# Convolution and mixture of experts on one core: the third round of fixed slots is merged into the per-expert tail

## The chip, the cores and the metric

The kernel runs on 1 core of one Trainium2 chip. The metric is device time in microseconds, the median of several runs. Besides, one execution is taken with the hardware profiler; its rows are what the prediction rests on. The span is the time from the first to the last instruction of that execution.

## The reference

What is computed is a causal depthwise convolution over the sequence (8 heads, 7 taps, taps made by a softmax) and then a mixture of 16 experts in 4 groups of 4, one expert per token:

```python
x = conv(x, softmax(weight))            # 8 x 2880 x 192 -> 23040 tokens of 192
g_idx = argmax(x @ w_group)             # group of each token, 4 groups
e_idx = argmax(xg @ w_expert[g])        # expert within the group, 4 experts
h  = maximum(xg[mask_e] @ w1[g, e], 0)  # 192 -> 1024
ye = h @ w2[g, e]                       # 1024 -> 192
out[tok_idx] = (g_w * e_w)[:, None] * ye
```

All is float32. The counts per expert are known only at run time; with the inputs here they lie between 1252 and 1628.

## The kernel before, in words

**Routing.** The 23040 tokens are routed in 25 units of 4 to 12 blocks of 120 tokens (`unit`). A unit convolves its tokens, writes rows of 196 values to `xcd` in HBM, computes logits and choices, and scatters the token numbers into per-expert lists in HBM (`idtab`, line 609). A unit is a Python generator; each `step` advances it by one small piece, so that routing work is put between the matmuls of the experts.

**Slots.** The expert work is a `plan` of slots. A slot takes up to 256 tokens of one expert: it gathers their rows by indirect DMA on POOL's queue (`gather`, line 674, one DMA per 128 rows, into one of four `xg` buffers), transposes them (`turn`, lines 689 and 690), multiplies with w1 (`hidden`, line 710) and w2 (`back`, lines 728 and 732), scales, and scatters into the output (`finish`, line 830, POOL's queue too). Each float32 operand is split in a rounded part and a remainder, so there are 5 matmuls per 128 hidden features and 2 per 128 rows and 128 features on the way back. ACT makes the rounded part, DVE the remainder.

**Portions and tail.** The plan before has three fixed portions, `portions = [(5, 1), (NU-6, 2), (NU, 1)]`: in the first, each expert has one slot of 256 rows (slots 0 to 15), which starts when 5 units are routed; in the second, two slots each (16 to 47); in the third, one slot each (48 to 63), which starts when all units are routed. What is left of each list goes to a tail of one entry per expert, the experts sorted by what they have left. An entry has a fixed shape (`PIECES`): pieces of 320, 384, 256 or 128 rows. The tail before holds 7040 rows in 25 pieces, from slot 64 to slot 88, in the order of `RANKS`. All in all 64 x 256 + 7040 = 23424 rows are computed.

**Pieces of the tail.** Pieces of 320 and 384 rows go through `hidden_wide` and `back_wide` (lines 787, 790, 793, 805, 811): the moving operand of w1's matmuls is 320 or 384 columns wide, each 128 features take a PSUM bank of their own, and the third row tile takes a bank of pool `pm`. Pieces of 128 rows go through `hidden_small`, `turn_small` and `back_small` (lines 746 to 772), which need extra transposes.

**Weights.** At each change of expert w1 and w2 are read again from HBM (`weights`, lines 623 to 626, SP's queue, 1.5 MB) and split (`split`, lines 638 to 651, on ACT and DVE).

**Opening.** `open_portion` reads the id lists of a portion (line 1070). For the last portion it also starts `open_tail`: the ends of the lists are padded (`close_table`, 16 writes at line 856, for which `seen` is made at line 849, an instruction kept in program order on DVE), the sorted table is computed on DVE, written and read back, and then the tail's ids are read (`tail_ids`, lines 1093 and 1095). `open_slot` advances this by one step per slot. `rate` sets how densely routing steps are put between matmuls: portion q's units are to be done `MARGIN` = 5 slots before that portion starts.

**Order.** Each engine and each DMA queue executes its instructions in the order in which the framework's scheduler put them. The scheduler works at build time from the program and its own estimate of when each instruction becomes ready, so that an instruction which waits for nothing by that estimate can stand far ahead of its place in the program. An instruction at the head of a queue whose input is not there holds everything behind it.

**In a slot** the order on TensorE is: first and second quarter of `hidden`, each followed by a part of the previous slot's `back`; the transposes for the next slot; then the third and fourth quarter of `hidden` in one run. The first matmul of that run is called the slot's mark below.

Of the kernel before, what the change touches and what calls it, by code (L numbers as in the profile page):

```python
# [35 lines left out]
def conv_moe_kernel(  # L36
# [20 lines left out]
    def pin(on, ins):  # L57
# [22 lines left out]
        [(320, 320)] * 2 + [(320, 256)] * 2 + [(256, 256)] + [(128, 320)] * 4 + [(384,)] * 3 + [(320,)] * 2 + [(256,)] * 2)  # L80
# [3 lines left out]
    RANKS = [5, 2, 6, 3, 7, 4, 8, 0, 9, 14, 1, 10, 12, 11, 13, 15]  # L84
    assert NTAIL == E and sorted(RANKS) == list(range(E)) and sorted(CAPS, reverse=True) == CAPS
# [18 lines left out]
    portions = [(NEED, 1), (NU - NEXT, 2), (NU, 1)]  # L104
# [12 lines left out]
    LAG_S = 2  # L117
# [162 lines left out]
    def clear_table():  # L280
        for h in range(2):
            pin(PINC1, nc.sync.dma_start(
                out=idtab[0:E * CAP, :].rearrange("(e r) c -> e (r c)", e=E)[:, h * LIM // 2:(h + 1) * LIM // 2],
                in_=fill[h * E:(h + 1) * E],
            ))
        pin(PINC2, nc.sync.dma_start(
            out=idtab[DUMMY:DUMMY + MOST, :].rearrange("(p r) c -> p (r c)", p=2), in_=fill[0:2, 0:MOST // 2],
        ))
# [325 lines left out]

    def weights(r1, r2, eng=None):
# [54 lines left out]
    def gather(ids, known, w=SLOT):  # L670
        xs = xg[nslot[0] % NXG]
        nslot[0] += 1
        for t, n in enumerate(split_rows(w)):
            nc.gpsimd.indirect_dma_start(  # L674
                out=xs[0:n, t, :], out_offset=None, in_=xcd[0:known, :],
                in_offset=bass.IndirectOffsetOnAxis(ap=ids[t].bitcast(U32), axis=0),
                bounds_check=known - 1, oob_is_err=False,
            )
# [58 lines left out]

    def hidden_small(W, X, h):
        xa, xb = X
        hp = ph.tile([P, 512], F32, name="ph")  # L740
        fs = slice(h * 512, (h + 1) * 512)
        xh, xl = xa[:, 0, 0:P], xa[:, 1, 0:P]
        ops = ((xh, W["ah"]), (xh, W["al"]), (xl, W["ah"]),
               (xb[:, 0, 0:P], W["bb"]), (xb[:, 1, 0:P], W["bb"]))
        for i, (xx, wgt) in enumerate(ops):
            nc.tensor.matmul(out=hp, lhsT=xx, rhs=wgt[:, fs], start=i == 0, stop=i == len(ops) - 1)
        hr = pa4.tile([P, UB, D2], F32, name="xcb").rearrange("p b d -> p (b d)")[:, 0:512]
        nc.scalar.activation(out=hr, in_=hp, func=AF.Relu)
        return hr

    def turn_small(hr):
        px = pm.tile([P, 512], F32, name="pm")
        for c in range(4):
            nc.tensor.transpose(px[:, c * P:(c + 1) * P], hr[:, c * P:(c + 1) * P], ident)
        hh = ff.tile([P, 2, SLOT], F32R, name="hh", bufs=HB).rearrange("p a b -> p (a b)")
        hl = ff.tile([P, 2, SLOT], F32R, name="hl", bufs=HB).rearrange("p a b -> p (a b)")
        nc.scalar.activation(out=hh, in_=px, func=AF.Copy)
        nc.vector.tensor_tensor(out=hl, in0=px, in1=hh.bitcast(F32), op=ALU.subtract)
        return hh, hl

    def back_small(W, oo, HH, h):
        hh, hl = HH
        cw = W["cw"]
        for c in range(4):
            f = 4 * h + c
            nc.tensor.matmul(
                out=oo[0][:, 0:2 * D], lhsT=hh[:, c * P:(c + 1) * P], rhs=cw[:, f].rearrange("p a d -> p (a d)"),
                start=f == 0, stop=False,
            )
        for c in range(4):  # L770
            f = 4 * h + c
            nc.tensor.matmul(
                out=oo[0][:, 0:D], lhsT=hl[:, c * P:(c + 1) * P], rhs=cw[:, f, 0, :], start=False, stop=f == NF - 1,
            )
# [263 lines left out]
    late = []  # L1038

    def open_tail():  # L1040
# [4 lines left out]
        for j in RANKS:  # L1045
            row = nc.values_load(
                tab[0][0:1, j, 2:3], engines=[ET.SP], min_val=0, max_val=DUMMY,
                skip_runtime_bounds_check_because=OOB_WHY,
            )
            tail_ids(row, idps["tail"][:, j], PIECES[j])  # L1050
            yield

    def open_portion(pi):
        need, spe = portions[pi]
        rows = spe * 2
        idp = const.tile([P, E, rows], I32, name=f"idp{pi}")
# [6 lines left out]
        else:  # L1063
# [42 lines left out]
    plan += [("tail", j, k) for j in RANKS for k in range(len(PIECES[j]))]  # L1106
# [4 lines left out]
    starts = {pi: i for i, (pi, e, s) in reversed(list(enumerate(plan))) if pi != "tail"}  # L1111

# [7 lines left out]
    assert not any(width(i) > SLOT and width(i + 1) < SLOT for i in range(len(plan) - 1))  # L1120

    def open_slot(i):
# [7 lines left out]
        while pi != "tail" and pi not in idps:  # L1130
# [6 lines left out]
        if late:  # L1137
            next(late[0], None)
# [107 lines left out]
    for i, (pi, e, s) in enumerate(plan):  # L1246
# [5 lines left out]
        n = min(w, SLOT) // P  # L1252
# [7 lines left out]
        oo = [po.tile([P, 512], F32, name="po") for _ in range(n)]  # L1260
        if w > SLOT:
            oo.append(None)
        steps = NF // 2 if n == 2 else 2
        for f2 in range(steps):
            last = f2 == steps - 1
            if w > SLOT:
                H2 = hidden_wide(W, turned[i], f2, w)

                def fold(W=W, oo=oo, H2=H2, f2=f2, w=w, xs=gathered[i], ids=ids, last=last):
                    if f2 == 0:  # L1270
                        oo[2] = pm.tile([P, 512], F32, name="pm")
                    back_wide(W, oo, H2, f2, w)
                    if last:
                        finish(oo, xs, ids, w)

                later(LAG - last, fold)
            elif n == 2:
                HH = hidden(W, turned[i], f2, lambda: advance(rate[0]))
                advance(rate[0])

                def fold(W=W, oo=oo, HH=HH, f2=f2, xs=gathered[i], ids=ids, last=last):
                    back(W, oo, HH, f2, lambda: advance(rate[0]))
                    if last:
                        finish(oo, xs, ids)

                later(LAG - last, fold)
            else:
                hr = hidden_small(W, turned[i], f2)

                def fold(W=W, oo=oo, hr=hr, f2=f2, xs=gathered[i], ids=ids, last=last):  # L1290
                    HH = turn_small(hr)

                    def fold2():
                        back_small(W, oo, HH, f2)
                        if last:
                            finish(oo, xs, ids, P)

                    later(LAG_S, fold2)

                later(0.5, fold)  # L1300
            if f2 == 0:
                open_slot(i + 2)
            for q in range(f2, NF // 2, steps):
                k = (q + 2) % 4
                if q < 2:
                    split_one(W, k)
                elif i + 1 < len(plan):
                    split_one(opened[i + 1][0], k)
            if i + 1 < len(plan):
                if f2 == n - 1:  # L1310
                    turned[i + 1] = turn(gathered[i + 1], width(i + 1))
# [30 lines left out]
```

## Time and profile before

| | |
|---|---|
| median of 3 runs | 1144.63 us (1143.6 to 1149.39) |
| profiled execution | 1137.87 us |
| its span | 1136.1 us |
| TensorE busy | 1087.7 us, 96% of the span |
| VectorE, ScalarE, GpSimd busy | 794.3, 719.6, 461.7 us |
| mean granted TensorE clock | 0.979 of full speed |
| DMA | 175.68 MB, mean 155 GB/s |

The profiled execution is 6.8 us shorter than the median of the runs, and its own time is 1.8 us more than its span. The rows below are all of this one execution. Times in them are microseconds from the span's start, "x" is a count, and a name such as L674 is a line of the program printed above.

### The profile page before, as it was taken

Reading aid. Unit: us, or ns where it says so; the run is one execution under the profiler, and the core shown is the slowest. Engines: PE = TensorE matmul, PEld = TensorE weight load, DVE = VectorE, ACT = ScalarE, POOL = GpSimd, SP = SyncE. Lnnn points to the kernel's source line nnn. Section 1 sums busy time; section 2 is a strip of 40 time slices with the busy share of each in tenths; the row PEclk is TensorE's granted clock in tenths of the full one; section 3 lists DMA queues with packets and bytes.
Section 4 is the critical chain, followed back from the end, with each engine's and each line's share of the span. In section 5 each row is a group of like instructions: output and inputs, shape, how many; then the busy total and the mean of one; then the engine's idle time right before and its main releaser. Section 6 shows DMA issues by size and latency. Waiting matters only on the chain. (4 is left out here: it accounts for less than half of the span.)

```text
span 1136.1 us, 23048 instructions
## 1 busy us (share of the span) xinstructions
PE 1087.7 (96%) x8170; PEld 1060.3 (93%) x8170; DVE 794.3 (70%) x1761; ACT 719.6 (63%) x1427; POOL 461.7 (41%) x420
## 2 busy tenths in 40 slices
PE   6799999999999999999999996999999999999995
PEld 5679899999999999999999996999999999999995
DVE  3747967887866666675678665888876766767772
ACT  4545576666775665656655664777776666666661
POOL 2003432234342534343435435555455454454531
PEclk9978999999999999999999998999999999999998
DMA  8879778879873564435354446777764444444420
GB/s 198 239 182 240 187 180 210 222 171 244 215 204 115 127 165 119 132 99 152 99 140 102 128 83 175 208 207 209 201 179 109 120 122 118 121 118 123 121 79 20
DMA packets 185203, 175.68 MB, mean 155 GB/s; under 512 B 47101, under 2 KB 166938, under 8 KB 185082
## 3 DMA queue, kind: packets, MB, share of 16 engines
q1 hardware_dynamic: 120108, 120.00, 39.2%
q0 software_dynamic: 18336, 36.08, 11.4%
q10 hardware_dynamic: 46638, 18.07, 7.4%
q8 instruction: 65, 1.06, 0.4%
q14 instruction: 56, 0.46, 0.1%
HBM read 138.23 MB, written 36.47 MB: 154 GB/s over the span
## 5 line engine op out<-in xcount | busy, mean ns | idle before, releaser
L728 PE MATMUL po<-cw,hh 128*128 128x384 f32 x1120 | 353.0, 372 | 0.4 <-ACT ys L822 0.4
L710 PE MATMUL ph<-xa,ah 128*128 128x256 f32 x1120 | 307.8, 296 | 4.4 <-DVEq L1190 2.4
L732 PE MATMUL po<-cw,hl 128*128 128x192 f32 x1120 | 281.2, 251 | 0.0
L715 ACT ACTIVATE hh<-ph 128x512 fp32r<-128x512 f32 x280 | 166.3, 595 | 162.7 <-PE ph L710 150.3
L674 POOL DMA_INDIRECT xg<-xcd,idp x128 | 143.1, 1118 | 306.6 <-ACT ys L822 275.6
L716 DVE SCALAR_TENSOR_TENSOR hl<-ph,hh 128x512 fp32r<-128x512 f32 x280 | 191.3, 686 | 92.9 <-ACT hh L715 89.7
L710 PE MATMUL ph<-xb,bb 128*128 128x256 f32 x1120 | 226.0, 283 | 0.0
L710 PEld LDWEIGHTS ph<-xa,ah 128*128 128x128 f32 x1120 | 212.3, 190 | 7.7 <-issue 2.7
L732 PEld LDWEIGHTS po<-cw,hl 128*128 128x128 f32 x1120 | 214.8, 192 | 1.9
L728 PEld LDWEIGHTS po<-cw,hh 128*128 128x128 f32 x1120 | 211.7, 189 | 2.9 <-ACT ys L822 0.6
L830 POOL DMA_INDIRECT out<-ys,idp x128 | 155.5, 1215 | 48.4 <-issue 30.1
L710 PEld LDWEIGHTS ph<-xb,bb 128*128 128x128 f32 x1120 | 173.2, 190 | 0.0
L710 PE MATMUL ph<-xa,al 128*128 128x256 f32 x560 | 158.3, 283 | 0.0
L822 ACT ACTIVATE ys<-po,xg 128x384 f32<-128x384 f32 x174 | 99.4, 581 | 77.2 <-PE po L732 41.5
L651 DVE TENSOR_TENSOR cw<-raw,cw 128x768 fp32r<-128x768 f32 x128 | 121.6, 952 | 19.3 <-ACT cw L650 17.4
L674 POOL DMA_INDIRECT xg<-xcd,idpt x61 | 69.2, 1135 | 136.7 <-ACT ys L822 95.2
L829 DVE TENSOR_TENSOR ys<-ys 128x192 f32<-128x192 f32 x177 | 62.6, 356 | 77.3 <-ACT ys L822 76.4
L650 ACT ACTIVATE cw<-raw 128x768 fp32r<-128x768 f32 x128 | 107.1, 842 | 4.2 <-DMA raw<-in_moe_w 4.1
L710 PEld LDWEIGHTS ph<-xa,al 128*128 128x128 f32 x560 | 107.5, 192 | 1.8
L639 DVE TENSOR_TENSOR al<-raw,ah 128x1024 fp32r<-128x1024 f32 x64 | 78.1, 1220 | 31.8 <-ACT ah L638 31.3
L830 POOL DMA_INDIRECT out<-ys,idpt x61 | 70.3, 1153 | 50.2 <-DVE ys L829 33.4
L638 ACT ACTIVATE ah<-raw 128x1024 fp32r<-128x1024 f32 x64 | 68.1, 1064 | 23.3 <-PE ph L710 10.1
(238 smaller groups left out, 1979.5 us busy)
## 6 DMA issues: line engine op xcount, KB each, us to landing
raw<-in_moe_w SPq DMA_DIRECT2D x128, 384.0 KB
raw<-in_moe_w SPq DMA_DIRECT2D x64, 512.0 KB
raw<-in_moe_w SPq DMA_DIRECT2D x64, 256.0 KB
xcd<-xc ACTq DMA_DIRECT2D x13, 742.5 KB
xin<-in_x SPq DMA_DIRECT2D x7, 1134.0 KB
xin<-in_x SPq DMA_DIRECT2D x6, 1039.5 KB
xcd<-xcb ACTq DMA_DIRECT2D x13, 360.0 KB
xg<-xcd,idp POOLq DMA_INDIRECT x128
```

Source lines behind the costliest of these rows:

```text
L638: pin(PINA, nc.scalar.activation(out=ah, in_=ra, func=AF.Copy))
L639: eng.get(k, nc.vector).tensor_tensor(out=al, in0=ra, in1=ah.bitcast(F32), op=ALU.subtract)
L650: pin(PINW, nc.scalar.activation(out=cw[:, fs, 0, :], in_=rc[k - 2], func=AF.Copy))
L651: eng.get(k, nc.vector).tensor_tensor(out=cw[:, fs, 1, :], in0=rc[k - 2], in1=cw[:, fs, 0, :].bitcast(F32), op=ALU.subtract,)
L674: nc.gpsimd.indirect_dma_start(out=xs[0:n, t, :], out_offset=None, in_=xcd[0:known, :], in_offset=bass.IndirectOffsetOnAxis(ap=ids[t].bitc ...
L710: nc.tensor.matmul(out=hp[:, j], lhsT=wgt[:, fs], rhs=xx, start=i == 0, stop=i == len(ops) - 1)
L715: nc.scalar.activation(out=hh, in_=hp, func=AF.Relu)
L716: nc.vector.scalar_tensor_tensor(out=hl, in0=hp, scalar=0.0, in1=hh.bitcast(F32), op0=ALU.max, op1=ALU.subtract,)
L728: nc.tensor.matmul(out=oo[t][:, 0:2 * D], lhsT=hh[:, j, ts], rhs=cw[:, f].rearrange("p a d -> p (a d)"), start=f == 0, stop=False,)
L732: nc.tensor.matmul(out=oo[t][:, 0:D], lhsT=hl[:, j, ts], rhs=cw[:, f, 0, :], start=False, stop=f == NF - 1,)
L822: nc.scalar.activation(out=y, in_=oo[t][0:n, 0:2 * D], func=AF.Copy, scale=g)
L830: nc.gpsimd.indirect_dma_start(out=outviews[nscat[0] % len(outviews)], out_offset=bass.IndirectOffsetOnAxis(ap=ids[t].bitcast(U32), axis=0 ...
```

## The change

The third fixed portion gets no slots of its own (`(NU, 0)`). Its 16 x 256 rows go into the tail, whose entries are now two or three pieces of 384, 320 and 256 rows, up to 896 rows per expert, 11136 rows in 36 pieces, from slot 48 to slot 83. Pieces of 128 rows and their functions are gone. The tail runs in order of size. The count of rows computed stays 48 x 256 + 11136 = 23424. The last portion now only closes the routing; its start is set to slot 48 - 8 = 40, so that routing is to end at slot 35, before 43. The tail's opening goes two steps per slot, and is forced on when a tail slot needs an id that is not read yet. The gather of a third row tile gets an order edge behind the gather of the second; the reads of the tail's ids get one behind the last w2 load issued so far.

```diff
     PIECES = (
-        [(320, 320)] * 2 + [(320, 256)] * 2 + [(256, 256)] + [(128, 320)] * 4 + [(384,)] * 3 + [(320,)] * 2 + [(256,)] * 2)
+        [(256, 384, 256)] * 2 + [(256, 320, 256)] * 2 + [(384, 384)] + [(384, 320)] * 4 + [(384, 256)] * 3
+        + [(320, 256)] * 2 + [(256, 256)] * 2)
...
-    RANKS = [5, 2, 6, 3, 7, 4, 8, 0, 9, 14, 1, 10, 12, 11, 13, 15]
...
-    portions = [(NEED, 1), (NU - NEXT, 2), (NU, 1)]
+    portions = [(NEED, 1), (NU - NEXT, 2), (NU, 0)]
+    LEAD = 8
...
-            hold(nc.sync.dma_start(
+            loads.append(nc.sync.dma_start(
                 out=rc[k], in_=w2f[bass.ds(r2 + k * HF * P, HF * P), :].rearrange("(f p) d -> p f d", p=P),
             ))
...
         for t, n in enumerate(split_rows(w)):
-            nc.gpsimd.indirect_dma_start(
...
+            with tc.issue_after(ins.ins) if t == 2 else nullcontext():
+                ins = nc.gpsimd.indirect_dma_start(
...
-        for j in RANKS:
-            row = nc.values_load(
...
-            tail_ids(row, idps["tail"][:, j], PIECES[j])
+        for j in range(NTAIL):
+            with tc.issue_after(loads[-1].ins):
+                row = nc.values_load(
...
+                tail_ids(row, idps["tail"][:, j], PIECES[j])
+            ready[0] = j + 1
             yield
...
-        else:
+        elif rows:
             ci = const.tile([1, E], I32, name=f"ci{pi}")
...
+    starts[len(portions) - 1] = len(starts) and plan.index(("tail", 0, 0)) - LEAD
...
-        if late:
-            next(late[0], None)
+        for _ in range(2):
+            if late:
+                next(late[0], None)
+        while pi == "tail" and ready[0] <= e:
+            next(late[0])
...
-        steps = NF // 2 if n == 2 else 2
-        for f2 in range(steps):
+        for f2 in range(NF // 2):
...
-                H2 = hidden_wide(W, turned[i], f2, w)
+                HH = hidden_wide(W, turned[i], f2, w, lambda: advance(rate[0]))
```

## Rows read from the trace of the kernel before

**Rows 1.** The page, part 1: busy us, share of the span, instructions, of each engine.

```profile
PE 1087.7 (96%) x8170; PEld 1060.3 (93%) x8170; DVE 794.3 (70%) x1761; ACT 719.6 (63%) x1427; POOL 461.7 (41%) x420
```

**Rows 2.** Windows by stage: stretch, length, busy us and records per engine, clock, DMA.

```profile
142.00:340.00 198.00, 197.57 (x1563) 191.65 (x1563) 152.49 (x315) 139.53 (x279) 74.30 (x65) 1.00 0.84 207
340.80:596.40 255.60, 255.60 (x2028) 252.36 (x2027) 169.88 (x351) 154.37 (x302) 101.86 (x93) 1.00 0.48 128
...
624.80:681.60 56.80, 56.80 (x445) 56.80 (x444) 38.06 (x62) 37.25 (x68) 22.06 (x20) 1.00 0.46 106
...
716.12:823.55 107.43, 107.43 (x838) 107.43 (x837) 90.44 (x132) 82.24 (x144) 55.76 (x43) 1.00 0.70 202
833.10:1023.17 190.07, 188.87 (x1313) 184.42 (x1311) 128.85 (x289) 126.42 (x252) 94.23 (x83) 1.00 0.44 124
```

**Rows 3.** Waits of PE over the span: what for, us in total, times, longest.

```profile
PE pm L689 <- DMA xg<-xcd,idp: 9.3, 2, 7.5
...
PE ph L710 <- DVEq L1190: 2.4, 1, 2.4
...
PE ph L787 <- DVE xc L793: 2.0, 7, 0.7
```

**Rows 4.** Timeline of POOL: start, us, instruction, idle before it and what ended it.

```profile
606.31 0.97 POOL L609 DMA_INDIRECT idtab<-lsi,rowi  x1 [2.29 <-DVE lsi L607]
...
686.14 0.99 POOL L674 DMA_INDIRECT xg<-xcd,idpt  x1 [14.83 <-DMA idpt<-idtab]
689.07 1.74 POOL L674 DMA_INDIRECT xg<-xcd,idpt  x1 [1.94 <-DMA idpt<-idtab]
691.11 1.02 POOL L674 DMA_INDIRECT xg<-xcd,idp  x1 [0.30 <-issue]
```

**Rows 5.** Timeline of SP's DMA queue, 590 to 712 us.

```profile
662.35 15.53 SPq L856 DMA_DIRECT2D idtab<-seen  x16
682.56 0.36 SPq L1093 DMA_DIRECT2D idpt<-idtab  x1
```

**Rows 6.** Waits of all engines, 660 to 715 us.

```profile
ACT cw L650 <- DMA raw<-in_moe_w: 4.1, 2, 2.1
```

**Rows 7.** Timeline of PE: the marks of slots 49, 50, 51 and 62, and two transposes.

```profile
685.28 0.30 PE L710 MATMUL ph<-xa,ah 128*128 128x256 f32 x1
...
694.30 0.33 PE L689 MATMUL pm<-ident,xg 128*128 128x128 f32 x1 [1.79 <-DMA xg<-xcd,idp]
...
702.21 0.47 PE L689 MATMUL pm<-ident,xg 128*128 128x128 f32 x1 [7.46 <-DMA xg<-xcd,idp]
...
706.33 0.30 PE L710 MATMUL ph<-xa,ah 128*128 128x256 f32 x1
...
716.12 0.30 PE L710 MATMUL ph<-xa,ah 128*128 128x256 f32 x1
...
823.55 0.30 PE L710 MATMUL ph<-xa,ah 128*128 128x256 f32 x1
```

**Rows 8.** Timeline of PE: marks in the tail (256 four times, 384 twice).

```profile
833.10 0.30 PE L710 MATMUL ph<-xa,ah 128*128 128x256 f32 x1
...
874.44 0.29 PE L710 MATMUL ph<-xa,ah 128*128 128x256 f32 x1
...
915.55 0.29 PE L710 MATMUL ph<-xa,ah 128*128 128x256 f32 x1
...
953.53 0.30 PE L710 MATMUL ph<-xa,ah 128*128 128x256 f32 x1
...
1061.00 0.35 PE L787 MATMUL ph<-xa,ah 128*128 128x384 f32 x1
...
1089.01 0.34 PE L787 MATMUL ph<-xa,ah 128*128 128x384 f32 x1
```

**Rows 9.** Groups by line, forms apart, DVE, 994 to 1108 us: busy us, mean ns.

```profile
L793 DVE SCALAR_TENSOR_TENSOR xc<-ph,xc 128x384 fp32r<-128x384 f32 x24 | 12.8, 552 | 4.5 <-ACT xc L790 4.1
...
L716 DVE SCALAR_TENSOR_TENSOR hl<-ph,hh 128x512 fp32r<-128x512 f32 x4 | 2.7, 686 | 1.6 <-ACT hh L715 1.6
```

More of the change, by code (lines that the diff above doesn't have):

```diff
@@ L1 @@
-from contextlib import ExitStack
+from contextlib import ExitStack, nullcontext
 import concourse.bass as bass
@@ L612, in unit @@
         finished(u)
+    loads = []
     def weights(r1, r2, eng=None):
@@ L735, in back @@
             hook()
[L738 to L774, printed above, removed]
     def hidden_wide(W, X, f2, w, hook=lambda: None):
@@ L1038, in conv_moe_kernel @@
     late = []
+    ready = [0]
     def open_tail():
@@ L1055, in open_portion @@
         rows = spe * 2
-        idp = const.tile([P, E, rows], I32, name=f"idp{pi}")
+        idp = rows and const.tile([P, E, rows], I32, name=f"idp{pi}")
         if pi == 0:
@@ L1105, in conv_moe_kernel @@
     plan = [(pi, e, s) for pi, (_, spe) in enumerate(portions) for e in range(E) for s in range(spe)]
-    plan += [("tail", j, k) for j in RANKS for k in range(len(PIECES[j]))]
+    plan += [("tail", j, k) for j in range(NTAIL) for k in range(len(PIECES[j]))]
     weights_at = {}
@@ L1129, in open_slot @@
                 open_portion(closing.pop())
-        while pi != "tail" and pi not in idps:
+        while (len(portions) - 1 if pi == "tail" else pi) not in idps:
             step()
@@ L1259, in conv_moe_kernel @@
             rare()
-        oo = [po.tile([P, 512], F32, name="po") for _ in range(n)]
-        if w > SLOT:
-            oo.append(None)
-        steps = NF // 2 if n == 2 else 2
-        for f2 in range(steps):
-            last = f2 == steps - 1
-            if w > SLOT:
-                H2 = hidden_wide(W, turned[i], f2, w)
-                def fold(W=W, oo=oo, H2=H2, f2=f2, w=w, xs=gathered[i], ids=ids, last=last):
+        oo = [po.tile([P, 512], F32, name="po") for _ in range(2)] + [None] * (w > SLOT)
@@ L1270, in fold @@
+        for f2 in range(NF // 2):
+            last = f2 == NF // 2 - 1
+            if w > SLOT:
+                HH = hidden_wide(W, turned[i], f2, w, lambda: advance(rate[0]))
+            else:
+                HH = hidden(W, turned[i], f2, lambda: advance(rate[0]))
+            advance(rate[0])
+            def fold(W=W, oo=oo, HH=HH, f2=f2, w=w, xs=gathered[i], ids=ids, last=last):
+                if w > SLOT:
                     if f2 == 0:
                         oo[2] = pm.tile([P, 512], F32, name="pm")
-                    back_wide(W, oo, H2, f2, w)
@@ L1273, in fold @@
[L1273 to L1281, printed above, removed]
-                    back(W, oo, HH, f2, lambda: advance(rate[0]))
[L1283 to L1300, printed above, removed]
+                    back_wide(W, oo, HH, f2, w, lambda: advance(rate[0]))
+                else:
+                    back(W, oo, HH, f2, lambda: advance(rate[0]))
@@ L1301, in conv_moe_kernel @@
+                if last:
+                    finish(oo, xs, ids, w)
+            later(LAG - last, fold)
             if f2 == 0:
                 open_slot(i + 2)
[L1303 to L1308, printed above, removed]
+            if f2 < 2:
+                split_one(W, f2 + 2)
+            elif i + 1 < len(plan):
+                split_one(opened[i + 1][0], f2 - 2)
```

23 lines of the change are left out of this document (10 added, 13 removed).

## The prediction

> **What bounds the kernel now.** I read the engines' shares first: TensorE (PE) is busy 96% of the span, the next engine 70% [rows 1]. PE sets the time, so a term of the sum must be either PE work that goes or PE idle time that goes. Then the table by stage. In the routing stages PE is busy 197.57 of 198.00 us and 255.60 of 255.60 us, in the slots 48 to 63 after a disturbance 107.43 of 107.43, in most of the tail 188.87 of 190.07 [rows 2]. So what isn't PE work sits in few places. The list of PE's waits names them: 9.3 us for two gathers, 2.4 us at the branch before the last slot, 2.0 us in seven short waits in the wide pieces (the longest 0.7) [rows 3]. The start of the kernel also has idle time, which the change doesn't reach.
>
> The 9.3 us are one event. The timeline of POOL shows at 686.14 a gather with tail ids (idpt) that had held the queue for 14.83 us until these ids landed, then another that held it for 1.94, and only then, at 691.11, the next gather with ordinary ids [rows 4]. Those ids are needed from slot 64 on, 14 slots later; the gathers stood early in the queue because nothing else held them back: a third row tile of an `xg` buffer has no earlier user. The ids were late because SP's queue was writing the 16 paddings from 662.35 for 15.53 us and read the first tail ids at 682.56 [rows 5]. Behind the two gathers stood those of slot 51, for which PE waits at the transposes 1.79 and 7.46 us [rows 7].
>
> **The change part by part.** The sum is made on the profiled execution, 1137.87 us, and its difference is carried to the median of 1144.63, which is 6.8 us higher.
>
> *Third tiles in order.* A slot undisturbed takes (823.55 - 716.12) / 11 = 9.77 us from mark to mark. From slot 49's mark to slot 50's it takes 706.33 - 685.28 = 21.05 [rows 7]. The event costs 21.05 - 9.77 = 11.28 us, of which 9.25 are the two waits; the other 2.0 go with the matmuls after them, which run at a lower granted clock (the transpose at 702.21 takes 0.47 us, that at 694.30 0.33). With the edge, a third tile's gather stands behind the second's, and that one waits for its buffer, so it can't run ahead. What is late next there is nothing in the rows: slots 51 to 62 run without a wait. **Term: -11.3 us.** Bounds: 0 (it stays) and -11.3.
>
> *Other pieces for the same rows.* 23424 rows in both. Before: 70 pieces of 256 (64 slots and 6), 12 of 320, 3 of 384, 4 of 128. After: 65, 8, 11 and none. So 5 x 256, 4 x 320 and 4 x 128 go, and 8 x 384 come (3072 rows each way). The prices come from marks in the tail [rows 8]. The order there is 128, 320, 320, 256 twice, then 128, 320, 256, 256. The first two groups take 41.34 and 41.11 us, the third 37.98. From the third, 128 + 320 cost 37.98 - 2 x 9.77 = 18.44. From the first two, 82.45 - 2 x 9.77 - 2 x 18.44 = 26.03, so 320 costs 13.0 (and 128 costs 5.4). Between two marks of 384 lie one 384 and one 320: 28.01 - 13.0 = 15.0 for 384. These prices have the waits of the tail in them. Removed: 5 x 9.77 + 4 x 18.44 = 122.6. Added: 8 x 15.0 = 120.0. **Term: -2.6 us.** A 384 is thus no cheaper by row than a 256 (1.5 x 9.77 = 14.65); what is gained is the dear 128s, with their extra transposes. Bounds: with 384 at 14.65, -5.4. On the other side, if each of the 19 wide pieces after met the longest wait seen, 0.7 us, instead of the mean of 2.0 / 15 = 0.13, 19 x 0.57 = 10.8 more, which gives +8.2. I take the marks, since they are the same pieces on the same engine.
>
> Against this stands a rule of the Trainium skill (VectorE: DVE Perf Modes, section "The TRN2 errata"): an operation has a fixed cost, so tiles should have 512 elements or more. What rows show first: DVE's remainder takes 686 ns for 512 columns and 552 for 384 [rows 9], so a 256 costs DVE 4 x 0.686 = 2.7 us of its 9.77, a 384 costs 8 x 0.552 = 4.4 of its 15.0, 28% and 29%. The rule shows in the price of one instruction, and by it alone the wide pieces would be the dearer ones, which is the third rival below; by the rows the load by time stays level.
>
> *Sixteen reloads of weights go* (25 MB, 16 times four loads on SP and eight splits on ACT and DVE). They lie beside PE: with a reload at each slot PE needs 107.43 / 838 = 128.2 ns for a matmul record, with one at each second slot 56.80 / 445 = 127.6 [rows 2]. The difference is 0.05 us a slot (76 records), 0.7 us for 16. **Term: -0.7.** Bounds 0 and -0.7.
>
> *Routing ends at slot 35 instead of 43.* The same PE work, denser: the last units are spread over 24 slots instead of 32. In the stage from 142 to 340 us routing is denser than it will be anywhere later (DVE is busy 77% there, 66% in the next), and PE is kept busy all the same [rows 2]. **Term 0**; the cover is that PE has work in any case. If that cover is gone, I have only the idle share of the denser stage, 0.43 of 198 us, as a price: under 0.6 us.
>
> *The tail's opening moves with it*, 16 paddings (15.53 us of SP's queue [rows 5]), the table on DVE, 32 id reads. Behind them on SP stand the weight loads. In the profile that block makes ACT wait 4.1 us for w2 [rows 6], and no PE wait for a weight follows [rows 3]; that was with a reload at each slot, while the block now falls on slots with one at each second, so the cover is wider. The 16 id reads of the third portion go from the same queue. The order edge behind w2 holds an id read until that load is issued; who waits for an id read is the gathers on POOL, and behind these all gathers and scatters. What it takes to be in time is the last rival. **Term 0**, bounds 0 and that rival's price.
>
> *Two gathers and two scatters fewer on POOL, 80 matmuls fewer on the w1 side:* within the prices above. *The end* (branch, last slot of 256, last scatter) stays, with its 2.4 us.
>
> Sum: -11.3 - 2.6 - 0.7 = -14.6 us, the profiled execution 1123.3, the median **1130**.
>
> **The rivals.**
>
> *The wait stays or comes back with the new first tail pieces.* The rows name the buffer, not the row tile, so that the two early gathers were third tiles is my reading of the program. If they weren't, or if other gathers take their place, only -2.6 - 0.7 is left: 1141.3. For it: the queue still mixes gathers whose ids come by two ways. Against it: a first or second tile has to wait for its buffer's earlier user. Chance 0.11.
>
> *The wide pieces are dear.* The upper bound above, 10.8 us: 1141. For it: 10 of the new wide pieces come one after the other (384, 384 and four times 384, 320), with splits of weights on DVE in the middle, and it is DVE that PE waits for [rows 3]. Against it: the same mix at 1061 to 1089 us is already in the price of 15.0. Chance 0.12.
>
> *Slower: the tail's ids come too late for slot 48.* Before, the third portion stood between the end of routing and the tail. From the last list scatter at 606.31 to the first gather with tail ids at 686.14 [rows 4] it takes 79.8 us. Slot 51's gather came to the head of POOL's queue at 686.14 - 14.83 = 671.3, 33 us ahead of that slot's undisturbed mark (685.28 + 2 x 9.77 = 704.8). So slot 48 needs the lists done 79.8 + 33 = 113 us, 11.6 slots, ahead: by slot 36.4. The plan is slot 35, and two steps per slot instead of one shorten the chain, whose longest part is the padding that waits for its place in the program. If routing ended where it does now, 69 us ahead of slot 48's mark (685.28 - 9.77 = 675.5), POOL would be held 44 us. PE had about 10 us of cover (19.8 us late on POOL, 9.3 idle on PE), so it would lose 34: 1164. It gets slower than before by over 0.5% when PE loses 14.6 + 5.7 = 20.3 us, which is a list done after slot 39.6. Chance 0.06.
>
> **How the numbers follow.** 0.5%, 5.7 us, is about what a measurement of this kernel can tell from no change. Forecast 0.71 (1123 to 1138), the wait stays 0.11, wide pieces dear 0.12, ids late 0.06. Low end: all bounds at their best, 11.3 + 5.4 + 0.7 = 17.4, and the fastest run shown being 1.0 below the median, give 1126; 1.2 us of PE idle in the tail [rows 2] and the scheduler's new order elsewhere can add a little, so 1123. High end: the two rivals at 1141. That leaves out the late ids and the tails of the rest, under 0.2. Faster by over 0.5% means under 1138.9: the forecast and half of the dear wide pieces, 0.77. Within it: the rest of these and the wait that stays, 0.17. Slower: 0.06.
>
> **What would show it.** Right: no gather with tail ids holds POOL for more than a few us, and PE's wait for gathers in the middle is gone; the stage after slot 48 needs about 15.0 us for a 384 and 9.77 for a 256; the paddings on SP stand some 60 to 110 us ahead of the first tail slot; PE's wait L787 for DVE is 2 to 4 us in all. Wrong: a hole in PE's 40 slices at the first tail pieces or at the end of routing; a wait of PE for weights after SP's block; a price of 384 over 15.5.

## The result, and the profile after

The changed kernel takes 1135.73 us (median, 1132.99 to 1136.54) beside 1147.01 for the kernel before. The ratio on record for this pair is 0.9874, interval [0.9825, 0.9922]; the quotient of the two medians, 0.9902, lies within it. Against the 1144.63 of the prediction, 1130 was forecast, a ratio of 0.9872. The experiments e1 to e4, e5 to e8 and e9 to e12 ran on a chip each; on the first and the last of these the ratio came out as 0.9841 [0.9808, 0.9873] and 0.9824 [0.9792, 0.9857]. So the kernel is faster, by 1.3 to 1.8% as these ratios have it. These ratios leave out one slow execution of e2, which took 4218.45 us. The size is near the forecast, though the last interval lies wholly on the faster side of it; most of the steps to it are not, as the experiments show.

The table of PE's waits of the changed kernel (what for, us in total, times, longest) has no row for gathers of 9.3 us any more [rows 3]:

```profile
PE ph L752 <- DVE xc L758: 6.4, 13, 1.1
...
PE ph L713 <- DVE hl L719: 3.3, 3, 2.1
...
PE ph L713 <- DVEq L1161: 1.0, 1, 1.0
```

L752, L713 and L1161 answer to L787, L710 and L1190 of before. POOL's timeline has the last list scatter and the first gather with tail ids [rows 4]:

```profile
538.29 0.96 POOL L609 DMA_INDIRECT idtab<-lsi,rowi  x1 [1.77 <-DVE lsi L607]
...
660.44 1.05 POOL L677 DMA_INDIRECT xg<-xcd,idpt  x1 [4.05 <-ACT ys L787]
```

No gather waits for tail ids now: the first that uses them waited for ACT's scaling of an earlier slot (`ys`, L787), which still read its buffer, and not for a DMA. The paddings stand at 578.45 on SP's queue and the first id read at 597.23, 98 and 80 us ahead of the first tail slot's transposes at 676.77 [rows 5]:

```profile
578.45 10.66 SPq L821 DMA_DIRECT2D idtab<-seen  x16
597.23 0.36 SPq L1061 DMA_DIRECT2D idpt<-idtab  x1
```

And yet this profiled execution spans 1134.3 us, only 1.8 less than the 1136.1 of before, with PE as busy as it was [rows 1]:

```profile
PE 1087.8 (96%) x8054; PEld 1060.3 (93%) x8054; DVE 728.8 (64%) x1652; ACT 666.5 (59%) x1338; POOL 453.0 (40%) x416
```

The reading needs stages. I cut each span at the first transpose for slot 5 and at that for slot 48 (the first slot of the third portion before, the first tail slot after; the rows left to compute are the same), in microseconds:

| kernel | up to slot 5 | slot 5 to 48 | slot 48 to end | span |
|---|---|---|---|---|
| before | 161.5 | 501.6 | 473.0 | 1136.1 |
| changed | 172.8 | 504.0 | 457.5 | 1134.3 |
| before again (e1) | 163.4 | 501.7 | 469.1 | 1134.2 |
| changed again (e2) | 163.4 | 502.6 | 451.1 | 1117.0 |
| before with the edge (e3) | 165.8 | 501.0 | 470.4 | 1137.2 |
| changed without the edge (e4) | 167.2 | 502.6 | 451.1 | 1120.9 |
| changed, routing late (e5) | 163.0 | 514.8 | 451.6 | 1129.3 |
| before, routing early (e6) | 162.3 | 514.8 | 459.7 | 1136.8 |
| before, early and edge (e7) | 164.8 | 506.1 | 461.4 | 1132.3 |
| changed, wide piece last (e8) | 162.2 | 502.8 | 448.6 | 1113.5 |
| changed, one weight load (e9) | 166.9 | 503.1 | 446.6 | 1116.6 |
| changed, table on GpSimd (e10) | 167.9 | 504.3 | 451.5 | 1123.7 |
| both (e11) | 170.0 | 503.5 | 452.9 | 1126.4 |
| changed again (e12) | 169.3 | 503.0 | 453.6 | 1125.9 |

The first profile of the changed kernel lost 11.3 us up to slot 5, where the order of PE's instructions is that of before. In e2, the same program, this part takes 163.4. It is a matter of the execution (more on it in the last section); the medians are over several executions. From slot 48 on the change saves 15.5 us in the first pair and 18.0 in the second; slots 5 to 48 cost 2.4 and 0.9 more.

### The profile page after: what moved, and what is told of

Same layout as the page of the kernel before. It is cut to its first block, busy times and chain, and to the rows that moved or that the text cites. A ratio compares the mean times of both kernels' runs of the same rounds, so it can differ in the third digit from the quotient of the medians.

```text
span 1134.3 us, 22263 instructions
## 1 busy us (share of the span) xinstructions
PE 1087.8 (96%) x8054; PEld 1060.3 (93%) x8054; DVE 728.8 (64%) x1652; ACT 666.5 (59%) x1338; POOL 453.0 (40%) x416
## 4 chain that ended last, share of the span: by engine, by line
PE 78%; DVE 6%; DMA 6%; issue 4%; ACT 3%; POOL 1%; another core or an unknown queue 1%; SPq 0%; POOLq 0%; ACTq 0%
PE ph L713 24%; PE po L731 15%; PE ph L752 8%; PE po L735 7%; PE po L770 4%; PE pm L437 4%; PE pm L485 2%; PE pm L770 2%; PE po L776 2%; DMA out<-ys,idpt 2%; PE pm L692 2%; DMA raw<-in_moe_w 2%; PE pm L693 2%; PE pm L455 1%; PE pm L480 1%
## 5 line engine op out<-in xcount | busy, mean ns | idle before, releaser
L731 PE MATMUL po<-cw,hh 128*128 128x384 f32 x1040 | 328.0, 372 | 1.1 <-ACT ys L787 1.1
L713 PE MATMUL ph<-xa,ah 128*128 128x256 f32 x1040 | 289.0, 298 | 6.2 <-DVE hl L719 3.3
L719 DVE SCALAR_TENSOR_TENSOR hl<-ph,hh 128x512 fp32r<-128x512 f32 x260 | 178.0, 688 | 138.2 <-ACT hh L718 121.5
L735 PE MATMUL po<-cw,hl 128*128 128x192 f32 x1040 | 261.0, 251 | 0.0
L677 POOL DMA_INDIRECT xg<-xcd,idp x96 | 110.3, 1149 | 260.0 <-ACT ys L787 228.7
L713 PE MATMUL ph<-xb,bb 128*128 128x256 f32 x1040 | 209.9, 284 | 0.0
L713 PEld LDWEIGHTS ph<-xa,ah 128*128 128x128 f32 x1040 | 198.8, 191 | 9.6 <-DVE hl L719 3.9
L677 POOL DMA_INDIRECT xg<-xcd,idpt x91 | 97.2, 1069 | 204.3 <-ACT ys L787 180.9
L713 PEld LDWEIGHTS ph<-xb,bb 128*128 128x128 f32 x1040 | 162.5, 192 | 0.0
L713 PE MATMUL ph<-xa,al 128*128 128x256 f32 x520 | 148.8, 286 | 0.0
L787 ACT ACTIVATE ys<-po,xg 128x384 f32<-128x384 f32 x168 | 96.3, 582 | 70.1 <-PE po L735 38.9
L795 POOL DMA_INDIRECT out<-ys,idp x96 | 116.0, 1208 | 39.6 <-issue 22.4
L795 POOL DMA_INDIRECT out<-ys,idpt x91 | 105.9, 1164 | 52.1 <-issue 28.3
L755 ACT ACTIVATE xc<-ph 128x384 fp32r<-128x384 f32 (+1 forms) x152 | 69.0, 468 | 84.5 <-PE ph L752 60.0
L758 DVE SCALAR_TENSOR_TENSOR xc<-ph,xc 128x256 fp32r<-128x256 f32 (+1 forms) x216 | 81.8, 415 | 54.9 <-ACT xc L755 49.4
L752 PE MATMUL ph<-xa,ah 128*128 128x384 f32 (+1 forms) x304 | 100.6, 334 | 6.4 <-DVE xc L758 6.4
L713 PEld LDWEIGHTS ph<-xa,al 128*128 128x128 f32 x520 | 99.9, 192 | 2.0
L653 DVE TENSOR_TENSOR cw<-raw,cw 128x768 fp32r<-128x768 f32 x96 | 91.5, 954 | 13.9 <-ACT cw L652 8.0
```

Of the source, the lines that this page charges most:

```text
L653: eng.get(k, nc.vector).tensor_tensor(out=cw[:, fs, 1, :], in0=rc[k - 2], in1=cw[:, fs, 0, :].bitcast(F32), op=ALU.subtract,)
L677: ins = nc.gpsimd.indirect_dma_start(out=xs[0:n, t, :], out_offset=None, in_=xcd[0:known, :], in_offset=bass.IndirectOffsetOnAxis(ap=ids[t ...
L713: nc.tensor.matmul(out=hp[:, j], lhsT=wgt[:, fs], rhs=xx, start=i == 0, stop=i == len(ops) - 1)
L719: nc.vector.scalar_tensor_tensor(out=hl, in0=hp, scalar=0.0, in1=hh.bitcast(F32), op0=ALU.max, op1=ALU.subtract,)
L731: nc.tensor.matmul(out=oo[t][:, 0:2 * D], lhsT=hh[:, j, ts], rhs=cw[:, f].rearrange("p a d -> p (a d)"), start=f == 0, stop=False,)
L735: nc.tensor.matmul(out=oo[t][:, 0:D], lhsT=hl[:, j, ts], rhs=cw[:, f, 0, :], start=False, stop=f == NF - 1,)
```

## The experiments

**Both kernels again.** No edit. 

> The kernel before, unchanged. Theory A (the 11.3 us by which the profile of after is behind at slot 5 is a matter of the execution, not of the change): the time by which the first transposes of slot 5 come is not 161.5 us again but up to 173, the rest of the span is as in the first profile (slot 48's transposes 501.6 us after slot 5's, the hole of some 21 us between the marks of slots 49 and 50 again), and the median of the runs stays 1143 to 1150. Rival B (the start is slower because of the change): slot 5's transposes stay at 160 to 163 us in this profile and the span at 1135 to 1138.

> The changed kernel, unchanged, for a narrower interval and a second profile. Theory A: ratio 0.986 to 0.990; in the profile slot 5's transposes come at any time from 161 to 173 us, and from slot 48's transposes to the end it takes 457 to 458 us. Rival B: slot 5's transposes at 172 to 174 us again.

Measured: 0.9987 [0.9964, 1.001] for the kernel before against itself, and 0.9841 for the change. The hole, as the stretch near slots 50 and 51 is called here in which PE stands and waits, is there in e1, on POOL (first fence) and on PE (second):

```profile
686.41 0.98 POOL L674 DMA_INDIRECT xg<-xcd,idpt  x1 [13.07 <-DMA idpt<-idtab]
```

```profile
700.73 0.48 PE L689 MATMUL pm<-ident,xg 128*128 128x128 f32 x1 [5.67 <-DMA xg<-xcd,idp]
```

From the transposes for slot 50 to those for slot 52 it takes 10.04 + 18.53 = 28.57 us in place of 2 x 9.76: the hole is worth 9.1 us here. So e1 to e2 is the cleanest pair: start 0.0, middle +0.9, from slot 48 on -18.0. The start does vary by itself (theory A). The 451.1 us of e2 from slot 48 on are fewer than the 457 to 458 expected: the first profile of the change has waits of ACT there (last section) that e2 doesn't have.

**The edge alone, and the change without it.**

```diff
+            with tc.issue_after(ins.ins) if t == 2 else nullcontext():
```

> The kernel before with the order edge for third row tiles alone; portions, pieces and routing as before. Theory (the edge takes the hole away, the prediction's term of 11.3 us): no gather with tail ids stands among those of slots 48 to 63, mark 49 to mark 50 takes 9.8 us, time 11.3 us under before, ratio 0.990. Rival (the hole is the padding's block of SP's queue, not the two gathers): PE still loses 5 to 11 us near slot 50 to weights that come late, ratio 0.995 to 1.000.

> The changed kernel without the order edge for third row tiles. Theory: third tiles of the first composites run ahead in POOL's queue, the first some 30 places before the first other tail gather, about 8 slots; it waits for ids that land at about 599 us, so POOL stands 10 to 20 us near 580 us and PE loses 5 to 12 us there; ratio 0.993 to 0.999. Rival (with the routing's end moved forward the ids are early enough, so the edge is worth nothing in this kernel): PE waits under 1 us for gathers, ratio 0.986 to 0.990.

Measured: e3 0.9995 [0.9975, 1.0014], e4 0.984 [0.9811, 0.9869], as much as the whole change. The edge does what it says and gains nothing. In e3 no gather with tail ids stands early in the queue, and the hole is still 5.2 us. SP's queue, ACT and PE in e3:

```profile
666.04 12.01 SPq L857 DMA_DIRECT2D idtab<-seen  x16
...
692.48 1.01 SPq L1094 DMA_DIRECT2D idpt<-idtab  x1
693.59 0.38 SPq L623 DMA_DIRECT2D raw<-in_moe_w  x1
```

```profile
697.46 1.06 ACT L638 ACTIVATE ah<-raw 128x1024 fp32r<-128x1024 f32 x1 [5.01 <-DMA raw<-in_moe_w]
```

```profile
703.45 0.39 PE L711 MATMUL ph<-xa,ah 128*128 128x256 f32 x1 [3.28 <-DVE hl L717]
...
847.29 0.33 PE L690 MATMUL pm<-ident,xg 128*128 128x128 f32 x1 [2.29 <-DMA xg<-xcd,idpt]
```

The paddings and the id reads behind them hold SP until 693; a w1 load comes out only then; ACT, at the head of whose queue the split of that weight stands, waits 5.01 us; behind it on ACT is the rounded part that DVE and then PE wait for. And the gathers that no longer run ahead are late at the tail's start: from one slot's transposes to the next it takes 16.80 us where e1 takes 12.76 (4.0 more). Hole and tail start together give back what the edge takes away. Of the two expectations the rival's came true.

In e4 the third-tile gathers do run ahead in the changed kernel, and one holds POOL:

```profile
591.53 1.04 POOL L677 DMA_INDIRECT xg<-xcd,idpt  x1 [11.15 <-DMA idpt<-idtab]
```

PE has no wait there, as the rival said. In the changed kernel the opening falls on slots of the second portion, which load weights at every second slot only, and the gathers are far enough ahead to bear 11 us.

**The routing's end.** e5 takes the lead away from the changed kernel, e6 gives it to the kernel before, e7 gives it lead and edge:

```diff
-    LEAD = 8
+    LEAD = 0
```

```diff
+    starts[len(portions) - 1] -= 8
```

> The changed kernel with LEAD = 0: routing is to end at slot 43 as before, all else as changed. Theory (the prediction's last rival: the tail's ids come too late for slot 48): the last list scatter comes some 70 us ahead of slot 48's mark instead of 137; from it to the first id read it took 59 us in the changed kernel, and the gather needs the ids 33 us ahead, so POOL is held 20 to 35 us and PE loses 10 to 25 us near slot 48; ratio to the kernel before 0.993 to 1.006. Rival (the end of routing has slack at 43 as well): no wait of PE for tail gathers, ratio 0.983 to 0.987.

> The kernel before with one line more: the third portion's start counts as slot 40, so that routing ends at slot 35; portions, pieces and gathers as before. Theory (the hole at slot 50 has two causes, one behind the other: gathers that wait for tail ids, and weights that are late behind the 16 paddings on SP; both come from the padding standing in the stage with a reload of weights at each slot): with the paddings 8 slots earlier the hole of 9 to 11 us is gone, ratio 0.990 to 0.993. Rival (the two gathers run ahead whatever the routing does): a hole of over 5 us moves to slots 40 to 45, ratio 0.996 to 1.000.

> The kernel before with the early end of routing and the order edge for third tiles. Theory: hole gone as in the run without the edge; what the edge alone gave back at the first tail pieces (the third tile's gather in line, 4 to 5 us near slot 64) is seen here again unless its ids are early; ratio 0.990 to 0.995, not better than without the edge. Rival (the edge is needed): clearly lower than without it.

Measured: e5 0.9955 [0.9939, 0.997], e6 0.9997 [0.9978, 1.0017], e7 0.9962 [0.9941, 0.9983]. In e5 a gather with tail ids stands at the head of POOL's queue (POOL's timeline):

```profile
608.07 0.97 POOL L609 DMA_INDIRECT idtab<-lsi,rowi  x1 [2.28 <-DVE lsi L607]
...
663.28 1.05 POOL L677 DMA_INDIRECT xg<-xcd,idpt  x1 [11.88 <-DMA idpt<-idtab]
```

But PE's one large wait, before the first tail slot's transposes at 677.74, is for an accumulator of `back` that ACT has to empty, and it isn't POOL that holds ACT (SP, then ACT, then PE):

```profile
644.66 10.76 SPq L821 DMA_DIRECT2D idtab<-seen  x16
660.73 0.36 SPq L1061 DMA_DIRECT2D idpt<-idtab  x1
661.62 0.36 SPq L625 DMA_DIRECT2D raw<-in_moe_w  x1
```

```profile
665.93 1.06 ACT L640 ACTIVATE ah<-raw 128x1024 fp32r<-128x1024 f32 x1 [12.33 <-DMA raw<-in_moe_w]
...
669.68 1.05 ACT L787 ACTIVATE ys<-po,xg 128x384 f32<-128x384 f32 x2
```

```profile
670.32 0.69 PE L731 MATMUL po<-cw,hh 128*128 128x384 f32 x1 [9.92 <-ACT ys L787]
```

The w1 load of the first tail entry stands on SP behind the paddings and the first id read, ACT waits 12.33 us for it, and what empties the accumulator (L787) comes after it on ACT. It is the chain of e3, longer. Slots 5 to 48 take 12.0 us more than in e8 on the same chip; PE has no wait for a gather with tail ids in this stretch. It might have had one: the first tail slot's gathers went out at 663.28 and 664.64, and its transposes were due at about 664.9 (from slot 47's transposes to these it takes 22.6 us in place of 9.76). That wait, if it is one, lies in the shadow of the weights'. In the changed kernel itself the w1 loads go out at 574.62, ahead of the paddings, and ACT has no wait for a weight there.

In e6 the hole moves with the opening, to slots 43 and 44, and stays (POOL, then PE):

```profile
610.89 0.99 POOL L674 DMA_INDIRECT xg<-xcd,idpt  x1 [12.25 <-issue]
```

```profile
621.88 0.33 PE L689 MATMUL pm<-ident,xg 128*128 128x128 f32 x1 [1.80 <-DMA xg<-xcd,idp]
...
635.50 0.48 PE L689 MATMUL pm<-ident,xg 128*128 128x128 f32 x1 [3.66 <-DMA xg<-xcd,idp]
```

These two slots take 8.5 us more than 2 x 9.76. POOL stood 12.25 us before a gather with tail ids; the trace names no releaser for it. So the theory of e6 failed and its rival held.

In e7 there is neither wait. So in the kernel before the hole goes only if the third tiles are held and the opening is moved. Why the move helps is read from how far ahead of the first transposes of its slot SP issues a w1 load: 14.3 us in slots 54 to 59 of the kernel before, which load at every slot, and 43.6 in slots 40 and 42 of the changed one, where every second slot loads. The first w1 load behind the block of paddings and id reads is still 2.45 us ahead in e3 (for slot 51), 40.1 in the changed kernel (for slot 44) and 24.5 in e7 (for slot 46; SP, then PE):

```profile
626.97 0.38 SPq L623 DMA_DIRECT2D raw<-in_moe_w  x1
```

```profile
651.45 0.27 PE L690 MATMUL pm<-ident,xg 128*128 128x128 f32 x1
```

In e5 the block stands in the same portion, but just ahead of the tail, and the load behind it was 3.3 us ahead of its slot. So few loads are not enough; what counts is that none is due soon behind the block. The order edge of the id reads behind a w2 load and the two steps per slot were not tried alone; e7 has neither and no hole.

That pair is worth 4.3 us (0.9962). In e7's profile 4.8 us of slots 5 to 48 are lost at slot 8, long before the opening (20.8 us, 15.9 in all other runs), so its stages show less than the 9.1 of the hole. The rest of the change's gain, 0.9962 to 0.984, is some 14 us by the ratios, which come from two chips. By the stages of e7 and e2 10.3 us of it fall to the merged tail, from slot 48 on; the other 3.5 lie before slot 48, where e7 lost its 4.8.

**The wide piece last in an entry.**

```diff
-        [(256, 384, 256)] * 2 + [(256, 320, 256)] * 2 + [(384, 384)] + [(384, 320)] * 4 + [(384, 256)] * 3
+        [(256, 256, 384)] * 2 + [(256, 256, 320)] * 2 + [(384, 384)] + [(384, 320)] * 4 + [(256, 384)] * 3
```

> The changed kernel with the wide piece as the last of an entry instead of the middle or first one (256, 256, 384; 256, 256, 320; 256, 384; 256, 320), same rows. Theory (the wide pieces came out cheaper than priced, 14.5 and 12.5 us instead of 15.0 and 13.0, because the splits of the next weights on DVE fall into 256 pieces): with the splits ah and bb in the wide pieces the nine entries cost 0.3 to 0.6 us more each, 3 to 5 us in all, ratio 0.987 to 0.989, and PE's wait L752 for DVE rises from 1.7 to over 4 us. Rival (the price depends on the width alone): ratio 0.983 to 0.985.

Measured: 0.983 [0.9804, 0.9856], not to be told from the change (0.984). The theory failed: PE's wait L752 falls to 0.9 us. By the stages the tail takes 448.6 us from slot 48 on, 2.5 less than in e2. Entries of three pieces take what they took. Those of two with one 256 got cheaper: (256, 384) 24.26 us where (384, 256) takes 24.46 in e2, and (256, 320) 22.29 where (320, 256) takes 23.13. The loads are the same. What moved is the place of their splits on DVE: of the four for each load, three (one of `bb` and the two of `cw`) have a remainder of the 256 next behind them (L719) in e8, and one of the wide piece (L758) in e2 (a split and what follows it, in e8 and then in e2):

```profile
1046.13 0.96 DVE L653 TENSOR_TENSOR cw<-raw,cw 128x768 fp32r<-128x768 f32 x1
1047.01 0.68 DVE L719 SCALAR_TENSOR_TENSOR hl<-ph,hh 128x512 fp32r<-128x512 f32 x1
```

```profile
1026.16 0.96 DVE L653 TENSOR_TENSOR cw<-raw,cw 128x768 fp32r<-128x768 f32 x1 [0.38 <-ACT cw L652]
1027.04 1.47 DVE L758 SCALAR_TENSOR_TENSOR xc<-ph,xc 128x256 fp32r<-128x256 f32 x6
```

**One weight load for the last eleven entries.** Their rows are computed with the weights of the fifth entry.

```diff
-            W = weights(...) if s == 0 else opened[i - 1][0]
+            W = weights(...) if s == 0 and e < 5 else opened[i - 1][0]
```

> The changed kernel without the weight loads and splits of the last 11 tail entries, which use the fifth entry's weights instead (so their rows get the wrong expert). In the changed kernel a 384 between two slots of 256 takes 14.5 us and a 320 there 12.5, 27.0 together, but the pair (384, 320), which has a load of weights within it, takes 27.53, and in the kernel before 384 and 320 with a load each take 28.0. Theory A: a load that falls on wide pieces costs PE about 0.5 us, since DVE's splits of weights stand in front of its remainders: the pairs go to 27.0, the entries (384, 256) from 24.46 to 24.27, in all -2.5 to -4 us against the changed kernel, ratio near 0.981. Theory B: it is two wide pieces in a row that cost the half microsecond: the pairs stay at 27.5, ratio that of the changed kernel, 0.984. Theory C (the prediction's): loads cost 0.04 us each wherever they fall, -0.5 us, pairs at 27.5.

Measured: the time, 0.9823 [0.9793, 0.9852], can't be told from that of e12 beside it, whose executions spread over 10 us. The stage can: from slot 48 on 446.6 us, against 451.1 (e2), 451.5 (e10) and 453.6 (e12). PE's transposes for four slots of 384, each a pair (384, 320) from the last, in e2 (first fence) and in e9 (second):

```profile
864.90 0.27 PE L692 MATMUL pm<-ident,xg 128*128 128x128 f32 x1
...
892.47 0.27 PE L692 MATMUL pm<-ident,xg 128*128 128x128 f32 x1
...
920.01 0.27 PE L692 MATMUL pm<-ident,xg 128*128 128x128 f32 x1
...
947.58 0.27 PE L692 MATMUL pm<-ident,xg 128*128 128x128 f32 x1
```

```profile
868.56 0.27 PE L692 MATMUL pm<-ident,xg 128*128 128x128 f32 x1
...
895.61 0.27 PE L692 MATMUL pm<-ident,xg 128*128 128x128 f32 x1
...
922.68 0.27 PE L692 MATMUL pm<-ident,xg 128*128 128x128 f32 x1
...
949.75 0.27 PE L692 MATMUL pm<-ident,xg 128*128 128x128 f32 x1
```

A pair takes 27.56 us with a load and 27.06 without. With two loads it took 28.01 in the kernel before [rows 8]. Each load that falls on wide pieces costs PE about half a microsecond in these pairs, theory A. Over the eleven loads taken away it is 4.5 us (e2 to e9), 0.4 each. Where it goes is seen in e2, on DVE and on PE:

```profile
898.11 0.96 DVE L653 TENSOR_TENSOR cw<-raw,cw 128x768 fp32r<-128x768 f32 x1
898.98 1.69 DVE L758 SCALAR_TENSOR_TENSOR xc<-ph,xc 128x384 fp32r<-128x384 f32 x3
```

```profile
898.99 0.36 PE L770 MATMUL po<-cw,xc 128*128 128x384 f32 x1
899.59 0.45 PE L752 MATMUL ph<-xa,ah 128*128 128x384 f32 x1 [0.24 <-DVE xc L758]
```

DVE splits a piece of w2 for 0.96 us, three remainders of the wide slot stand behind it, and PE's next matmul, due 0.2 us after the last start, comes after 0.6. In e9 PE's waits have no L752 row at all; in e2 they have eight, 1.7 us in all. This run takes away the transfers and ACT's splits too. That it is the order on DVE is shown by e8, which has every load: its (256, 384) and (256, 320) take 24.26 and 22.29 us, and in e9 (384, 256) and (320, 256) without a load take 24.27 and 22.29.

**The table's steps on GpSimd**, alone and with the wide piece last:

```diff
-                    ts(t["q"], t["rank"], k + 0.5, ALU.is_lt, float(XT), ALU.mult)
-                    tt(t["cap"], t["cap"], t["q"], ALU.add)
+                    nc.gpsimd.tensor_scalar(out=t["q"], in0=t["rank"], scalar1=k + 0.5, ...)
+                    nc.gpsimd.tensor_tensor(out=t["cap"], in0=t["cap"], in1=t["q"], op=ALU.add)
```

> The changed kernel with the 14 steps on capacities in the tail's table (two lines of the table, 16 values each) on GpSimd instead of DVE. Theory A: PE's 2.0 us wait for DVE's remainder at the end of routing, and the lower clock behind it, come from these DVE instructions standing in a block in front of the remainder: the wait goes to under 1 us, -2 to -3 us against the changed kernel, ratio near 0.9815. Rival: the other instructions of the table are enough to make the same wait, or the table is later and moves the paddings: 0 to -0.5 us, ratio 0.984.

> The changed kernel with the wide piece last in an entry and with the table's steps on GpSimd. If the two gains are independent (the first was 3 us, the second up to 3): 0.980 to 0.981; if the second is nothing: 0.983.

> The changed kernel once more, beside the other three on this chip, as the base for them: 0.984 as before; its table of PE waits and its 36 tail intervals as in its repeat. If the start up to slot 5 differs by several us again, that part is of the execution and not of the kernel.

Measured on one chip: e10 0.9859 [0.9821, 0.9896], e11 0.9841 [0.9812, 0.987], the unedited change (e12) 0.9824 [0.9792, 0.9857]. No gain. DVE and PE in e10:

```profile
533.17 0.29 DVE L858 TENSOR_SCALAR pos<-pos,tc_j,flags 128x16 f32<-128x16 f32 x1
538.06 0.17 DVE L861 TENSOR_TENSOR pos<-pos 128x16 f32<-128x16 f32 x1 [4.60 <-POOL pos L886]
```

```profile
539.51 0.39 PE L713 MATMUL ph<-xa,ah 128*128 128x256 f32 x1 [2.13 <-DVE hl L719]
```

The steps left DVE and the next step of the table stayed at the head of its queue, waiting 4.60 us for GpSimd with PE's remainder behind it. (The trace has twelve such steps, where the expectation counts 14.) It is the rival's result, but not by the cause that it names: what holds the remainder is not the rest of the table, but a step on DVE that needs the values from GpSimd. No version here beats the change beyond the intervals; e8 has the shortest span shown, 1113.5.

## Why the prediction was right, and where it was not

**The total held, its largest step did not.** The sum was -14.6 us: -11.3 for the edge, -2.6 for pieces, -0.7 for loads, 0 for the rest. From e1 to e2 the span loses 17.2: the hole -9.1, the branch before the last slot -1.5, pieces and loads together the rest of the -18.0, -7.4; the middle +0.9. That the total is near is in part luck: the hole went by another way than the one priced, and pieces and loads gave more than twice their terms. By the ratios the gain is some 14, 18 and 20 us (0.9874, 0.9841, 0.9824); by the medians of the first pair it is 11.3.

**Third tiles in order, -11.3.** The hole goes, but not by the edge: alone it gives 0 (e3), and the change does without it (e4). The step that failed is "What is late next there is nothing in the rows". The rows had it: ACT's 4.1 us for w2 behind SP's block [rows 6], which the opening's step set aside because "no PE wait for a weight follows". The waits of ACT in that same stretch of the kernel before, 660 to 715 us, have another row, which [rows 6] leaves out, for w1, the load on which e3's chain turns:

```profile
ACT ah L638 <- DMA raw<-in_moe_w: 3.3, 1, 3.3
```

No wait of PE followed because it was standing in the hole at that time, waiting for gathers. With the hole's first cause gone, the same block gave 5.01 us on ACT and 3.28 on PE. The hole had two causes, one in the shadow of the other, and another part of the change, the opening moved to where the next load is far ahead of its slot, is what removed the second. That step of the prediction ("so the cover is wider") was right in direction and priced at nothing; what it was worth is the part of the hole that is left in e3, 5.2 us, and gone in e7.

**Other pieces, -2.6, and loads, -0.7: -7.4 in e1 to e2.** From e7 to e2, with the hole out of both, it is -10.3 from slot 48 on, less 1.5 for the branch -8.8. The mis-sized term is the price of a wide piece. In e2 an entry (256, 384, 256) takes 34.03 us and (256, 320, 256) 32.07, less 2 x 9.77 it is 14.5 and 12.5, where 15.0 and 13.0 were taken. The marks of [rows 8] had a load of weights in nearly each wide piece, as the prediction said ("these prices have the waits of the tail in them") without asking which would stay. With 14.5 the same step gives 122.6 - 8 x 14.5 = -6.6. The 0.05 us for a load was read in slots of 256 and holds there (slots 43 to 48 take 9.76 us); on wide pieces a load costs eight to ten times that (e9), and the merged entries bring fewer: of the 19 wide pieces after, four stand between slots of 256 that take the splits, and ten share a load by pairs. The rule of the Trainium skill that the prediction weighed (VectorE: DVE Perf Modes, section "The TRN2 errata") would have made the wide pieces the dear ones; e9, with the same number of remainder operations of the same size and PE's waits gone, and e8, with the splits moved to the 256, show that the splits beside them were what cost. The Trainium skill states its advice there for operations that read SBUF; the remainder here reads PSUM as well.

**Routing earlier, 0: +0.9.** PE waits 2.0 us where the table stands in a block on DVE, a row that the prediction had no counterpart for. e10 did not remove it. How the +0.9 is made up isn't shown: e7 has the same wait, and its slots 5 to 48 less the 4.8 us of slot 8 take 501.3 us, no more than in e1. Behind the wait the granted clock fell in the first profile of the change: it is 0.66 as the mean of the next 5 us, of which 548 to 550 stand at 0.50, the lower of its two levels, and 551 on at 1.00. In e2 it stays at 1.00 behind a wait of the same length (first profile, then e2: stretch, length, busy us of the engines, clock, DMA):

```profile
547.00:552.00 5.00, 5.00 (x27) 4.93 (x27) 4.84 (x7) 1.62 (x4) 1.75 (x2) 0.66 0.45 63
```

```profile
537.60:542.60 5.00, 5.00 (x39) 5.00 (x40) 4.94 (x8) 2.89 (x7) 2.29 (x3) 1.00 0.48 82
```

**The end, "stays, with its 2.4 us".** It is 1.0. The last two pieces are now of one expert, with no load between them; which of the branch's inputs comes earlier by that wasn't tried.

**The rivals.** "The wait stays or comes back" is what happens with the edge alone in the kernel before: 5.2 us stay and 4.0 come back at the first tail pieces. "The wide pieces are dear" (the second rival; the paragraph on the Trainium skill calls it the third) is wrong in the repeats; in the first profile of the change PE's wait for them is 6.4 of the 10.8 us of its bound, but most of that by waits of ACT that e2 doesn't have (below). "The tail's ids come too late" has its case in e5, and is half right: with routing that ends where it did, the lead is missed and PE pays, but 12.0 us and not 34, and the wait that ends last is not for gathers. From the last list scatter to the first gather with tail ids it takes 663.28 - 608.07 = 55.2 us in e5 in place of the 79.8 of before, and POOL is held 11.88 us in place of 44. What PE waits for is the weight load that stands behind the same block on SP, which this rival had not named.

## What to carry to other kernels

A wait that the trace shows hides those that end in its shadow: before a hole is priced as a gain, list what else was late during it (other engines' waits in the same stretch), and try the one edit alone. A price read between marks carries the side work that fell on them; ask which of it comes along to the new place. A block of one-time transfers on the queue that loads weights is paid for by whoever waits for those loads. Here blocks of 10.8 to 12.0 us cost PE nothing in e2 and e7, 5.2 us in e3 and 12.0 in e5: what decided was whether a load behind the block was due soon.

## What the runs showed of the hardware

Up to slot 5 the executions take 161 to 173 us, with the same instructions of PE in the same order; the three profiles of the changed kernel itself take 172.8, 163.4 and 169.3. The rows that differ are PE's busy time and clock, in the stretch before slot 5 of the first profile of the change and then of e2 (columns as above):

```profile
131.50:172.79 41.29, 37.49 (x259) 34.34 (x257) 30.79 (x80) 22.57 (x46) 11.69 (x11) 0.88 0.63 172
```

```profile
128.10:163.37 35.27, 33.52 (x258) 31.38 (x257) 28.21 (x72) 21.93 (x45) 11.66 (x11) 0.95 0.70 190
```

With 259 and 258 records the one takes 6 us longer at a clock of 0.88 against 0.95. The 4.8 us of e7 at slot 8 are of the same kind: for 9 us the granted clock stands at 0.50, the lower of its two levels, while PE is busy throughout, and from 205 to 212 PE has no idle time either.

```profile
212.00:221.00 9.00, 9.00 (x36) 8.40 (x35) 5.10 (x15) 2.79 (x8) 2.04 (x2) 0.50 0.24 67
```

e6, whose slot 8 takes 15.9 us, has 1.00 there. What starts such a stretch wasn't tried.

In the first profile of the change ACT stands once per pair (384, 320) for 3.5 us before a rounded part, with no releaser in the trace, and PE after it (ACT, then PE):

```profile
875.55 1.25 ACT L755 ACTIVATE xc<-ph 128x384 fp32r<-128x384 f32 x3 [3.49 <-issue]
```

```profile
876.68 0.45 PE L752 MATMUL ph<-xa,ah 128*128 128x384 f32 x1 [1.10 <-DVE xc L758]
```

A pair then takes 28.9 us. e12 shows such waits in two pairs, e2 in none. Shorter ones (up to 2.7 us) stand in e9 to e11, so all four profiles from that chip have them before L755, and none of the changed kernels' from the chips of e1 to e8 has. The cause stays open.

On 128 x 16 values a pair of table steps takes 0.67 us on GpSimd (e10) and 0.42 on DVE (e2), from the starts of the rows.
